# Backward pass of a two-layer decoder step: a new order for the third turn of w1, a shorter regrouping and norm, and one turned tile kept

## Chip, cores and metric

The kernel runs on one core of one Trainium2 chip. The metric is the time of one execution in device microseconds; less is better.

## What is computed

The forward pass and all gradients of two equal layers with shared weights, for two sequences with one new token each. Cut to what matters:

```python
def _A_ref(x, k_cache, v_cache, wq, wo):            # attention, 32 heads on 4 kv heads, 16384 keys
    q = (x @ wq) ...
    p = _softmax(einsum("bhqd,bhkd->bhqk", q, k) * Dh ** -0.5)
    return einsum("bhqk,bhkd->bhqd", p, v) ... @ wo
def _B_ref(x, w1, b1, w2, b2):                      # mlp, D = 1024, F = 3584
    h = _gelu(einsum("bsd,df->bsf", _layernorm(x), w1) + b1)
    return einsum("bsf,fd->bsd", h, w2) + b2
x = x + _A_ref(_layernorm(x), ...); x = x + _B_ref(_layernorm(x), ...)     # layer 0
x = x + _A_ref(_layernorm(x), ...); x = x + _B_ref(_layernorm(x), ...)     # layer 1
# reference(): this output, and its vjp with respect to x, both caches and all weights
```

The caches are 2 x 4 x 16384 x 128 in bf16, 33.6 MB each. Each is read in the forward and in the backward pass of each layer, and a gradient of the same size is written for each.

## The kernel before, in words

All data that is larger than a vector travels in tiles of 128 partitions x 4096 bf16 (1 MB): a quarter of one head's keys or values (32 of 128 columns of keys), four row blocks of wq, wo or w2, or a piece of w1. The vectors of the two tokens are held as columns, 128 partitions x (blocks, 2).

The order of the work is a list written out by hand (`Program.emit`). Each entry names the tiles ("chunks") that it uses. `Program.run` walks through the list once and gives each chunk a slot: 16 slot tiles, and for a time parts of other buffers (two in `e1`, two in `ds1`, one in `late`). A load is issued on SyncE's queue as soon as the list has passed the last use of the slot that it gets; the loads are issued in the order of their first use. So a load waits in the queue for whoever last used its slot, and all later loads wait behind it. `Program.keep` leaves a tile in its slot between two uses where there is room. In the last attention's backward the slots change one after another into staging for outputs.

The stages: attention forward and mlp forward of layer 0, the same of layer 1, then backwards: mlp of layer 1, attention of layer 1, mlp of layer 0, attention of layer 0. In the last stage all the outputs are computed and stored: the gradients of both caches and of the weights, for both layers together, as outer products of 512 columns (`kv_outputs`, `dw_units`), whose PSUM results ScalarE (L276) and VectorE (L279) turn into bf16. `copy_bf` and `cast_out` choose between the two by running sums `st["act"]` and `st["dve"]`; `load_of("dve", 6.0)` adds 6 us to VectorE's sum, so that the next ones go to ScalarE.

A backward product needs the weights with rows and columns exchanged. VectorE's 32x32 transpose of pairs of bf16 ("turning", `turn_rows`, L437, and `turn_cols`, L473) does a quarter of this; the rest is done by a vector spread over four groups of 32 partitions (`spread`, L506 to L507) and 32-column products on the turned tile (`turned_products`, L487). The results then stand in four groups of 32 partitions, and `unquad` (L517 to L529) puts them in order: one copy out of PSUM and 16 small copies of 32 partitions, dealt out to VectorE, ScalarE and GpSimd in turn. Where there is time, weights are instead transposed in place by PE and ScalarE (`turn_here`, L452, L455) and used by plain products (`here_products`, L465).

w1 is turned twice. In the **second turn** (mlp of layer 1, at 415 to 442 us) whole rows are loaded, and `turn_cols` writes four tiles for each half of the rows: `w1t[h][cg]`, half h, column group cg of 896 columns. In the **third turn** (mlp of layer 0, at 633 to 662 us) w1 is loaded again as eight pieces `ws1c` (four row blocks x 896 columns, 896 KB), and `turn_rows` makes eight tiles of them, two halves each: `t1` is the list of the 16 turnings, `p1` the list of the eight product groups.

Around the third turn the list says, before: turnings 0 and 1 inside the attention backward's steps 135 and 137; after its end the last wq products, the layer norm's backward (`attn_in_bwd`: sums, close, rest), turnings 2 and 3, the 28 w2 products (L465) with turnings 4 to 8 among them, `dh0_` (L1533) with the spread, a copy that clears the tile Y (L1540), and then, after each product group, one output unit of w2's gradient (`first`: `y_rows` L1289, `x_rows` L1309, units L1326) and one or two turnings. Then `mlp_in_bwd` (sums, six units, rest), the eight wo products (`wo_prods0`), `do_of`, and the last attention's first steps.

The layer norm's backward (`ln_bwd_terms`, `ln_bwd_sums`, `ln_bwd_rest`) multiplies and sums per partition, sums over partitions with a product by ones (`part_sum`, L594), scales the sums by -1/D, and then needs three steps on (128, 8, 2) for the combination, one for the multiplication by rstd, one for the addition of the residual's gradient, and one for the bf16 copy.

The SyncE wait that the prediction speaks of belongs to `col_to_row` (L617, GpSimd's store): at step 111 of the attention backward of layer 1 the forward output is stored from a slot that a load takes next.

Of the kernel before, what the change touches and what calls it, by code (L numbers as in the profile page):

```python
# [18 lines left out]
LN_EPS = 1e-5  # L19
# [163 lines left out]
def kernel(  # L183
# [468 lines left out]
    def ln_bwd_terms(dy, y):  # L652
        t1 = wrk.tile([128, DJ, 2], F32, name="lb_t1")
        V.tensor_tensor(out=t1[:], in0=dy, in1=y, op=ALU.mult)
        s = small.tile([128, 2, 2], F32, name="lb_s")
        V.tensor_reduce(out=s[:, 0, :], in_=dy.rearrange("p j b -> p b j"), axis=AX.X, op=ALU.add)
        V.tensor_reduce(out=s[:, 1, :], in_=t1[:].rearrange("p j b -> p b j"), axis=AX.X, op=ALU.add)
        return flat(s[:])

    def ln_bwd_sums(dy, y, at=None):  # L660
        return part_sum(ln_bwd_terms(dy, y), 4, at)

    def ln_bwd_rest(ps, dy, y, rstd, twice=False):
        nm = small.tile([128, 2, 2], F32, name="lb_nm")
        V.tensor_scalar(out=flat(nm[:]), in0=ps, scalar1=-1.0 / D, scalar2=None, op0=ALU.mult)
        if twice:
            V.tensor_scalar(out=nm[:, 1, :], in0=nm[:, 1, :], scalar1=1.0 + LN_EPS, scalar2=None, op0=ALU.mult)
        u = wrk.tile([128, DJ, 2], F32, name="lb_u")
        V.tensor_tensor(out=u[:], in0=y, in1=bcast_j(nm[:, 1, :], DJ), op=ALU.mult)
        V.tensor_tensor(out=u[:], in0=u[:], in1=dy, op=ALU.add)  # L670
        V.tensor_tensor(out=u[:], in0=u[:], in1=bcast_j(nm[:, 0, :], DJ), op=ALU.add)
        dx = wrk.tile([128, DJ, 2], F32, name="lb_dx")
        V.tensor_tensor(out=dx[:], in0=u[:], in1=bcast_j(rstd, DJ), op=ALU.mult)
        return dx
# [248 lines left out]
    def mlp_in_bwd(l, fill, gT, parts=False):  # L923
        h = {}

        def sums():
            y, _ = saved[f"m{l}"]
            h["dm"] = wrk.tile([128, DJ, 2], F32, name="dm_sb")
            fill(h["dm"])
            h["ps"] = ln_bwd_sums(h["dm"][:], y[:], half[0, 0] if parts else None)  # L930

        def rest():
            y, r = saved[f"m{l}"]
            dx = ln_bwd_rest(h["ps"], h["dm"][:], y[:], r[:], True)
            gn = vec.tile([128, DJ, 2], F32, name=f"gM{l}")
            V.tensor_tensor(out=gn[:], in0=dx[:], in1=gT[:], op=ALU.add)
            V.tensor_copy(out=gA_all[:, :, 2 * l:2 * l + 2], in_=gn[:])
            return gn

        if parts:  # L940
            return sums, rest
        sums()
        return rest()
# [17 lines left out]
    def wo_bwd_ops(l, k, vb):  # L961
# [3 lines left out]
        def fin():  # L965
            raw = small.tile([128, 8, 2], F32, name="do_raw")
            unquad(raw[:].rearrange("p (c j) b -> p c j b", j=4), acc)
            V.memset(sb[0][:, 64:80], 0.0)
            dve(1.1)
            do_of(l, k, raw[:])  # L970
# [61 lines left out]
    def attn_bwd(l, order, gT, wo_first, outputs=None, mark=None, extra=None):  # L1032
# [127 lines left out]
        if l == 1:  # L1160
            todo = tail + parts
# [9 lines left out]
    def attn_in_bwd(l, gT, dnq):  # L1171
        h = {}

        def sums():
            dn = wrk.tile([128, DJ, 2], F32, name="dn")
            last = sb[0][:, 112:128].rearrange("p (j b) -> p j b", b=2)
            if l == 1:
                V.tensor_copy(out=dn[:], in_=last)
            else:
                V.tensor_tensor(out=dn[:], in0=last, in1=dnq[:], op=ALU.add)  # L1180
            h["dn"] = dn
            h["s"] = ln_bwd_terms(dn[:], vec_y[f"a{l}"][:])
            dve(0.8)

        def close():
            h["ps"] = part_sum(h["s"], 4, half[0, 0] if l == 1 else sb[0][:, 200:])

        def rest():
            dx = ln_bwd_rest(h["ps"], h["dn"][:], vec_y[f"a{l}"][:], vec_r[f"a{l}"][:])
            gn = saved[f"gA{l}"]  # L1190
            V.tensor_tensor(out=gn[:], in0=dx[:], in1=gT()[:], op=ALU.add)
            dve(1.3)
            if l == 1:
                V.tensor_copy(out=gM_all[:, :, 0:2], in_=gn[:])
# [295 lines left out]
    def g3_():  # L1490
        saved["g3"] = mlp_in_bwd(1, lambda dm: unquad(dm[:].rearrange("p (c j) b -> p c j b", j=4), dm_1), gT4)
# [27 lines left out]
    attn_bwd(1, up, lambda: saved["g3"], (None, wo_prods), mark=mark("d1"), extra=extra)  # L1519
# [20 lines left out]
    emit(lambda: S.copy(out=Y.ap.bitcast(I32), in_=wide["n"][:, 0:2].bitcast(I32).to_broadcast([128, CH // 2])), [Y])  # L1540
# [8 lines left out]
    g1p = mlp_in_bwd(0, lambda dm: unquad(dm[:].rearrange("p (c j) b -> p c j b", j=4), dm_0), g2, parts=True)  # L1549
# [47 lines left out]
    emit(lambda: load_of("dve", 6.0))  # L1597
# [49 lines left out]
```

## Time and profile before

| what | value |
|---|---|
| time, median of 3 runs | 1108.54 us (1106.45 to 1108.61) |
| the profiled execution's own time | 1104.69 us |
| its span on the core | 1102.9 us |
| mean granted TensorE clock | 0.927 |
| busy: PE, VectorE, ScalarE, GpSimd | 809.1, 759.6, 492.6, 181.7 us |
| DMA | 448.98 MB, mean 407 GB/s; loads and other hardware queue 351.32 MB, stores 95.48 MB |
| turnings of 128x896 in the third turn | 16, median 1.07 us each |
| loads of 896 KB | 24 by their lines: 16 whole rows of w1 and 8 pieces |

In the profile, a row names the line, the engine, the operation, the tile written and the tiles read, and how many there were. "idle before" is how long the engine did nothing ahead of it, with what ended that. The chain of waits runs back from the last instruction. SyncE does no arithmetic: its rows (SPq) are the issues of loads, and a late issue means that a slot was late. The busy table by stages gives, for each stretch, the busy time of the engines, the granted clock, the DMA engines' busy share and GB/s. Line numbers are those of the kernel before.

### The profile page before, as it was taken

To read this page: it belongs to the slowest core of one execution; us is meant where nothing else is said; L and a number is where in the kernel's file an instruction comes from. 1 tells how busy PE (TensorE), PEld (TensorE's weight loads), DVE (VectorE), ACT (ScalarE), POOL (GpSimd) and SP (SyncE) were. 2 spreads that over 40 slices of the span, in tenths; PEclk is the share of its full clock that TensorE was granted. 3 is DMA by queue.
4 is the path that set the end of the run, shared out by engine and by line. 5 is a ranking of instruction groups with operands and counts; after the bars stand their busy time and mean duration, and the time that the engine had idled before them with its cause. 6 is when DMAs were issued, how large, how long until landed. Compare 5 with 4: busy or idle time off the path is not lost. (4 is left out here: it accounts for less than half of the span.)

```text
span 1102.9 us, 34164 instructions
## 1 busy us (share of the span) xinstructions
PE 809.1 (73%) x14665; PEld 607.6 (55%) x14677; DVE 759.6 (69%) x1472; ACT 492.6 (45%) x1133; POOL 181.7 (16%) x575
## 2 busy tenths in 40 slices
PE   5665666457788657688778678878876986598795
PEld 4554565456777556688778564444443443344453
DVE  5864665168888637755746466979876896598974
ACT  0332222101242321235534326767675776477874
POOL 1000000001000000111211101433332332233330
PEclk9999999999999999988978657989997999799998
DMA  9999999999999999999999998999999999999996
GB/s 372 420 423 421 421 425 423 397 385 413 416 422 421 422 420 383 419 418 421 416 421 419 389 413 307 366 400 424 419 420 425 423 419 422 425 411 420 411 423 269
DMA packets 97932, 448.98 MB, mean 407 GB/s; under 512 B 7624, under 2 KB 11742, under 8 KB 59380
## 3 DMA queue, kind: packets, MB, share of 16 engines
q1 hardware_dynamic: 80532, 351.32, 78.2%
q0 software_dynamic: 17248, 95.48, 21.0%
q8 instruction: 115, 1.88, 0.6%
q14 instruction: 37, 0.30, 0.1%
HBM read 348.15 MB, written 98.62 MB: 405 GB/s over the span
## 5 line engine op out<-in xcount | busy, mean ns | idle before, releaser
L537 DVE STREAM_TRANSPOSE kT<-slot 128x512 int32<-128x512 int32 x436 | 294.1, 695 | 109.5 <-PE sc L550 90.9
L550 PE MATMUL sc<-qbd,kT 128*128 128x32 bf16 x4096 | 263.0, 222 | 11.0 <-DVE kT L537 10.2
L550 PEld LDWEIGHTS <-kT 128*128 128x128 bf16 x4096 | 209.1, 115 | 65.3 <-issue 33.4
L575 PEld LDWEIGHTS <-slot 128*128 128x128 bf16 x3456 | 141.9, 103 | 101.4 <-issue 45.3
L575 PE MATMUL sb<-xt,slot 128*128 128x8 bf16 x3456 | 157.6, 177 | 45.7 <-DMA slot<-in_A_v_cache_dram 23.9
L276 ACT CAST slot<-sc 128x512 bf16<-128x512 f32 x281 | 160.8, 594 | 58.2 <-PE sc L1326 25.0
L1266 PE MATMUL sc<-slot,late 128*128 128x512 bf16 x344 | 127.8, 392 | 23.3 <-DVE slot L279 10.0
L279 DVE CAST slot<-sc 128x512 bf16<-128x512 f32 x172 | 115.2, 678 | 24.5 <-PE sc L1326 10.4
L768 ACT ACTIVATE e<-sc 128x512 bf16<-128x512 f32 x32 | 19.0, 597 | 234.8 <-DVE sc L765 168.6
L276 ACT CAST slot<-sb 128x512 bf16<-128x512 f32 x151 | 89.6, 593 | 37.0 <-PE sb L1326 25.3
L455 ACT COPY slot<-tp 128x512 int32<-128x512 int32 x88 | 50.4, 587 | 106.0 <-PE tp L452 90.3
L452 PE MATMUL tp<-ident,slot 128*128 128x128 bf16 x768 | 74.4, 260 | 11.0 <-DMA slot<-in_A_wq_dram 5.7
L585 ACT COPY xt<-e 32x128 int32<-32x128 int32 x256 | 75.6, 295 | 3.9
L1266 PEld LDWEIGHTS <-late 128*128 128x128 bf16 x512 | 44.5, 98 | 59.5 <-issue 45.7
L1266 PE MATMUL sb<-slot,late 128*128 128x512 bf16 x162 | 63.7, 393 | 7.6 <-DVE slot L279 1.9
L1326 PE MATMUL sc<-slot,late 128*128 128x512 bf16 x155 | 58.7, 401 | 13.8 <-DVE slot L279 9.9
L452 PEld LDWEIGHTS <-slot 128*128 128x128 bf16 x768 | 60.1, 119 | 13.6 <-issue 6.3
L437 DVE STREAM_TRANSPOSE slot<-slot 128x1024 int32<-128x1024 int32 (+1 forms) x46 | 52.9, 1178 | 18.6 <-DMA slot<-in_A_wo_dram 9.1
L279 DVE CAST slot<-sb 128x512 bf16<-128x512 f32 x80 | 54.1, 677 | 9.5 <-PE sb L1266 6.2
L645 POOL TENSOR_TENSOR m_rstd<-ln_vpe,neghalf 128x2 f32<-128x2 f32 x2 | 1.4, 719 | 349.0 <-DVE ln_vpe L643 349.0
L585 POOL COPY xt<-late 32x64 int32<-32x64 int32 x240 | 55.6, 232 | 13.0 <-DVE late L1054 1.9
L585 POOL COPY xt<-ds 32x64 int32<-32x64 int32 x128 | 29.7, 232 | 148.5 <-DVE ds L1054 113.9
(298 smaller groups left out, 1090.9 us busy)
## 6 DMA issues: line engine op xcount, KB each, us to landing
slot<-in_A_k_cache_dram SPq DMA_DIRECT2D x103, 1024.0 KB, 16.4
slot<-in_A_v_cache_dram SPq DMA_DIRECT2D x101, 1024.0 KB, 16.0
out_dram<-slot POOLq DMA_DIRECT2D x55, 1024.0 KB, 14.3
slot<-in_A_wq_dram SPq DMA_DIRECT2D x25, 1024.0 KB, 12.4
slot<-in_A_wo_dram SPq DMA_DIRECT2D x25, 1024.0 KB, 19.7
out_dram<-slot POOLq DMA_DIRECT2D x40, 512.0 KB, 14.1
slot<-in_B_w_dram SPq DMA_DIRECT2D x22, 896.0 KB, 16.4
slot<-in_B_w_dram SPq DMA_DIRECT2D x12, 1024.0 KB, 12.8
```

The lines of the kernel that those rows point to most:

```text
L276: S.copy(out=dst, in_=src)
L279: V.tensor_copy(out=dst, in_=src)
L437: V.transpose(out=t.ap[:, h * nw * 256:(h + 1) * nw * 256].bitcast(I32).rearrange("p (w j m) -> p w j m", j=4, m=32), in_=c.ap[:, 0:4 * nc ...
L452: PE.transpose(tp[:, j * 128:(j + 1) * 128], c.ap[:, off + j * 128:off + (j + 1) * 128], ident[:])
L455: S.copy(out=d.bitcast(I32), in_=tp.bitcast(I32))
L537: V.transpose(out=kT[:].bitcast(I32).rearrange("p (w j m) -> p w j m", w=4, j=4), in_=c.ap[:, (i % 4) * 1024:(i % 4 + 1) * 1024].bitcast(I ...
L550: PE.matmul(sc[:, a0:a0 + 4, :, 2 * (i % 4) + q], lhsT=kv[:, 2 * q + w, :, e], rhs=qbd[:, q_at(g), 2 * w + e], start=(w == 0 and e == 0), ...
L575: PE.matmul(acc, lhsT=c.ap[:, n * 128:(n + 1) * 128], rhs=xv[:, i // 4, t // 2, :, 2 * (i % 4) + t % 2], start=(fresh and i == 0 and t == ...
L585: (GP.tensor_copy if on[t % len(on)] == "g" else S.copy)(out=d[32 * t:32 * t + 32, c0:c0 + cn, j, :], in_=s[32 * j:32 * j + 32, c0:c0 + cn ...
L768: S.activation(out=e_of(l, g)[:, 8 * f:8 * f + 8].rearrange("p a h b -> p h a b"), in_=sc[f][:].rearrange("p h (a b) -> p h a b", b=8), fu ...
L1266: PE.matmul(ps, lhsT=hold["blk"][:, j, :], rhs=flat(qm(w)[:, hf * 4:hf * 4 + 4, :]), start=True, stop=True)
L1326: PE.matmul(ps, lhsT=hold[j // 4 * 4][:, j % 4, :], rhs=Y.ap[:, y_at + c0:y_at + c0 + cn], start=True, stop=True)
```

## The change

- **The third turn in a new order.** Only one turning (one half of the first piece) stands in the attention backward, behind its last step and ahead of the wq products (`after`). Two follow the norm, three stand among the w2 products; the Y copy stands ahead of them; `y_rows` and two turnings stand behind the spread ahead of the first product group, and then one turning follows each of the first six groups.
- **One tile kept.** The tile `w1t[1][3]` of the second turn is used in the last product group of the third turn, too: seven pieces are loaded and turned, 14 turnings instead of 16. The tile keeps its slot from the second turn to the third.
- **A shorter regrouping.** `regroup` takes the place of `unquad` in both `mlp_in_bwd` and in `wo_bwd_ops`: one VectorE multiplication by `quad` out of PSUM, which spreads each value to its place and puts zeros elsewhere, and four f32 products with `quadT` (128 x 32), each into 32 partitions of a PSUM bank. `unquad` stays for `dh_last` and `dn_kept`.
- **A shorter norm.** The terms are multiplied by rstd first, the factor -1/D stands in the matrix of the product (`mean`), the residual's gradient is added while the sum is under way, and behind the sum there are two steps and one for each result (the bf16 one first).
- **Units moved.** Three units instead of six stand between the norm's two parts; one comes behind the wo products and two behind `do_of`. The `load_of("dve", 6.0)` ahead of the last attention goes.

```diff
+    quadT = vec.tile([128, 32], F32, name="quadT")
+    V.tensor_reduce(out=quadT[:], in_=identf[:].rearrange("p (a t) -> p t a", a=4), axis=AX.X, op=ALU.add)
+    mean = vec.tile([128, 1], F32, name="mean")
+    V.memset(mean[:], -1.0 / 1024)
+    meanf = mean[:].to_broadcast([128, 128])
...
+    def regroup(src, at):
+
+        C = src.shape[1]
+        q = small.tile([128, 8, 4, 2], F32, name="uq", bufs=1)[:, 0:4 * C]
+        V.tensor_tensor(out=q, in0=src.rearrange("p c a b -> p (c a) b").unsqueeze(2).to_broadcast([128, 4 * C, 4, 2]),
+                        in1=quad[:].unsqueeze(1).unsqueeze(3).to_broadcast([128, 4 * C, 4, 2]), op=ALU.mult)
+        ps = at[:, 0:8 * C].rearrange("p (c n) -> p c n", c=C)
+        qa = q.rearrange("p (c a) j b -> p c a (j b)", a=4)
+        for a in range(4):
+            PE.matmul(ps[32 * a:32 * a + 32], lhsT=quadT[:], rhs=qa[:, :, a], start=True, stop=True)
+        return ps.rearrange("p c (j b) -> p (c j) b", b=2)
...
+    def ln_bwd_terms(dy, y, rstd, gT, twice=False):
+
+        dr = wrk.tile([128, DJ, 2], F32, name="lb_dr")
+        V.tensor_tensor(out=dr[:], in0=dy, in1=bcast_j(rstd, DJ), op=ALU.mult)
         t1 = wrk.tile([128, DJ, 2], F32, name="lb_t1")
-        V.tensor_tensor(out=t1[:], in0=dy, in1=y, op=ALU.mult)
+        V.scalar_tensor_tensor(out=t1[:], in0=dr[:], scalar=1.0 + LN_EPS if twice else 1.0, in1=y, op0=ALU.mult, op1=ALU.mult)
...
+    def ln_bwd_sums(dr, s, gT, at=None):
+
+        ps = (ob() if at is None else at)[:, 0:4]
+        PE.matmul(ps, lhsT=meanf, rhs=s, start=True, stop=True)
+        V.tensor_tensor(out=dr[:], in0=dr[:], in1=gT, op=ALU.add)
+        return ps
+
+    def ln_bwd_rest(ps, dr, y, outs):
+
         u = wrk.tile([128, DJ, 2], F32, name="lb_u")
...
+        V.tensor_tensor(out=u[:], in0=y, in1=bcast_j(ps[:, 2:4], DJ), op=ALU.mult)
+        V.tensor_tensor(out=u[:], in0=u[:], in1=dr[:], op=ALU.add)
+        for out in outs:
+            V.tensor_tensor(out=out, in0=u[:], in1=bcast_j(ps[:, 0:2], DJ), op=ALU.add)
...
         if l == 1:
-            todo = tail + parts
+            todo = list(after) + tail + parts
...
     for n, c in enumerate(ws1c):
-        t = P.chunk()
-        t1 += turn_rows(c, t, 896)
+        t = w1t[n // 4][n % 4] if n == 7 else P.chunk()
+        t1 += [] if n == 7 else turn_rows(c, t, 896)
...
-    for n, b in enumerate(t1[0:2]):
-        extra.setdefault(135 + 2 * n, []).append(b)
...
-    for b in t1[2:4]:
+    emit(lambda: S.copy(out=Y.ap.bitcast(I32), in_=wide["n"][:, 0:2].bitcast(I32).to_broadcast([128, CH // 2])), [Y])
+    for b in t1[1:3]:
         emit(*b)
...
-        if j % 4 == 3 and 4 + j // 4 < 9:
-            emit(*t1[4 + j // 4])
+        if j % 4 == 3 and j < 12:
+            emit(*t1[3 + j // 4])
...
+    for b in first[0:1] + t1[6:8]:
+        emit(*b)
     for n, b in enumerate(p1):
         emit(*b)
-        for u in first[n + (n > 0):n + 2] + t1[max(9, 8 + 2 * n):10 + 2 * n]:
+        for u in first[n + 1:n + 2] + t1[8 + n + max(0, n - 5):9 + n + max(0, n - 4)]:
             emit(*u)
...
-    for u in first[9:15]:
+    for u in first[9:12]:
         emit(*u)
...
+    wo_prods0 = wo_prods0[:-1] + first[12:13] + wo_prods0[-1:] + first[13:15]
...
-    emit(lambda: load_of("dve", 6.0))
     attn_bwd(0, down, lambda: saved["g1"], (va0, wo_prods0), outputs=outputs, extra=extra)
```

More of the change, by code (lines that the diff above doesn't have):

```diff
@@ L657, in ln_bwd_terms @@
         V.tensor_reduce(out=s[:, 1, :], in_=t1[:].rearrange("p j b -> p b j"), axis=AX.X, op=ALU.add)
[L658 to L667, printed above, removed]
-        u = wrk.tile([128, DJ, 2], F32, name="lb_u")
[L669 to L674, printed above, removed]
+        return dr, flat(s[:]), gT
@@ L921, in mlp_in, with mlp_in_bwd @@
         saved[f"m{l}"] = (y, r)
-    def mlp_in_bwd(l, fill, gT, parts=False):
+    def mlp_in_bwd(l, src, gT, parts=False):
         h = {}
         def sums():
[L927 to L930, printed above, removed]
+            y, r = saved[f"m{l}"]
+            dm = regroup(src, half[0, 1] if parts else ob())
+            h["dr"], s, g = ln_bwd_terms(dm, y[:], r[:], gT[:], True)
+            h["ps"] = ln_bwd_sums(h["dr"], s, g, half[0, 0] if parts else None)
         def rest():
             y, r = saved[f"m{l}"]
-            dx = ln_bwd_rest(h["ps"], h["dm"][:], y[:], r[:], True)
             gn = vec.tile([128, DJ, 2], F32, name=f"gM{l}")
-            V.tensor_tensor(out=gn[:], in0=dx[:], in1=gT[:], op=ALU.add)
-            V.tensor_copy(out=gA_all[:, :, 2 * l:2 * l + 2], in_=gn[:])
+            ln_bwd_rest(h["ps"], h["dr"], y[:], [gA_all[:, :, 2 * l:2 * l + 2], gn[:]])
             return gn
@@ L965, in fin @@
         def fin():
-            raw = small.tile([128, 8, 2], F32, name="do_raw")
-            unquad(raw[:].rearrange("p (c j) b -> p c j b", j=4), acc)
+            raw = regroup(acc, ob())
             V.memset(sb[0][:, 64:80], 0.0)
-            dve(1.1)
-            do_of(l, k, raw[:])
+            dve(0.3)
+            do_of(l, k, raw)
         return turned_pair(ld_wo(k), acc, vb), (fin, ())
@@ L1030, in wq_last_ops, with attn_bwd @@
         return turns, prods
-    def attn_bwd(l, order, gT, wo_first, outputs=None, mark=None, extra=None):
+    def attn_bwd(l, order, gT, wo_first, outputs=None, mark=None, extra=None, after=()):
         kvs = []
@@ L1174, in sums @@
         def sums():
-            dn = wrk.tile([128, DJ, 2], F32, name="dn")
             last = sb[0][:, 112:128].rearrange("p (j b) -> p j b", b=2)
-            if l == 1:
-                V.tensor_copy(out=dn[:], in_=last)
-            else:
+            if l == 0:
+                dn = wrk.tile([128, DJ, 2], F32, name="dn")
                 V.tensor_tensor(out=dn[:], in0=last, in1=dnq[:], op=ALU.add)
-            h["dn"] = dn
-            h["s"] = ln_bwd_terms(dn[:], vec_y[f"a{l}"][:])
+                last = dn[:]
+            h["dr"], h["s"], h["g"] = ln_bwd_terms(last, vec_y[f"a{l}"][:], vec_r[f"a{l}"][:], gT()[:])
             dve(0.8)
         def close():
-            h["ps"] = part_sum(h["s"], 4, half[0, 0] if l == 1 else sb[0][:, 200:])
+            h["ps"] = ln_bwd_sums(h["dr"], h["s"], h["g"], half[0, 0] if l == 1 else sb[0][:, 200:])
         def rest():
-            dx = ln_bwd_rest(h["ps"], h["dn"][:], vec_y[f"a{l}"][:], vec_r[f"a{l}"][:])
             gn = saved[f"gA{l}"]
[L1191 to L1194, printed above, removed]
+            ln_bwd_rest(h["ps"], h["dr"], vec_y[f"a{l}"][:], ([gM_all[:, :, 0:2]] if l == 1 else []) + [gn[:]])
+            dve(0.8)
         res = [(sums, ()), (close, ()), (rest, ())]
@@ L1490, in g3_ @@
     def g3_():
[L1491 removed]
+        saved["g3"] = mlp_in_bwd(1, dm_1, gT4)
     emit(g3_)
@@ L1539 @@
     mark(-1)()
-    emit(lambda: S.copy(out=Y.ap.bitcast(I32), in_=wide["n"][:, 0:2].bitcast(I32).to_broadcast([128, CH // 2])), [Y])
     emit(lambda: load_of("dve", 6.0))
```

7 lines of the change are left out of this document (3 added, 4 removed).

## The prediction

> **What bounds the kernel now.** I read the page's 40 slices first, then the busy times stage by stage, then SyncE's and VectorE's timelines of 595 to 730 us. The DMA engines are 0.9 busy or more in 38 slices of 40, so time can only be won where they run dry or move slowly.
>
> ```profile
> DMA  9999999999999999999999998999999999999996
> GB/s 372 420 423 421 421 425 423 397 385 413 416 422 421 422 420 383 419 418 421 416 421 419 389 413 307 366 400 424 419 420 425 423 419 422 425 411 420 411 423 269
> ```
>
> The deepest dip inside the kernel is slice 25 (307 GB/s, 662 to 689 us): the third turn and what follows it. By stages (columns: stretch and its length; busy us of PE, weight loads, VectorE, ScalarE, GpSimd; granted clock, DMA share, GB/s):
>
> ```profile
> 650.00:662.00 12.00, 10.04 (x246) 8.54 (x245) 8.53 (x10) 5.97 (x9) 1.31 (x3) 0.50 1.02 425
> 662.00:668.00 6.00, 3.82 (x31) 1.80 (x31) 2.67 (x17) 4.15 (x12) 1.64 (x6) 0.50 1.01 413
> 668.00:676.00 8.00, 6.03 (x102) 4.96 (x101) 4.34 (x12) 2.96 (x7) 0.73 (x1) 0.50 1.01 391
> 676.00:684.00 8.00, 7.46 (x73) 3.55 (x70) 4.89 (x8) 7.50 (x17) 0.72 (x2) 0.98 0.34 76
> 692.00:717.00 25.00, 22.88 (x238) 11.55 (x238) 23.24 (x37) 20.15 (x39) 9.38 (x28) 1.00 0.96 359
> 730.00:1080.00 350.00, 283.06 (x3449) 153.99 (x3457) 276.41 (x476) 243.55 (x489) 118.74 (x349) 0.93 1.02 420
> ```
>
> Until 676 the DMA is full, from 676 to 684 it does almost nothing, from 692 to 717 PE (22.88 of 25) and VectorE (23.24) are the bound, and from 730 to 1080 the DMA is again (420 GB/s, share 1.02). SyncE's timeline says why (start, duration, line, load):
>
> ```profile
> 601.84 0.38 SPq L378 DMA_DIRECT2D slot<-in_A_wq_dram  x1
> 609.61 0.33 SPq L373 DMA_DIRECT2D slot<-in_A_v_cache_dram  x1
> ...
> 659.42 0.38 SPq L378 DMA_DIRECT2D slot<-in_A_wo_dram  x1
> 669.31 0.33 SPq L373 DMA_DIRECT2D slot<-in_A_v_cache_dram  x1
> 680.98 0.33 SPq L373 DMA_DIRECT2D slot<-in_A_k_cache_dram  x1
> 688.61 0.38 SPq L378 DMA_DIRECT2D slot<-in_A_wo_dram  x1
> ```
>
> All slots are full by 659. The next come free only as the last attention backward starts, at the end of this chain: the last K tile arrives (635.43), norm, w2 products (641.49), spread, w1 products (651.25 to 661.70), regrouping and norm (to 666.56), wo products (667.39), first V transposes (671.74). Whatever shortens the chain moves the stage up to 717 forward, and with it the full DMA stretch to the end, whose work is the same. Loads taken away before 676 win nothing by themselves: they make the DMA run dry sooner.
>
> **The change, part by part**, against the profiled execution: 1104.69 us, span 1102.9.
>
> *Start of the chain.* One w1 load (896 KB) goes, the first moves behind the last K tile: 0.9175 MB at the 403 to 408 GB/s of 632 to 640 us is 2.27 us earlier for K. But the kept tile takes a slot from the second turn to the third, so all loads in between are issued one release later. Mostly the queue hides that: bytes issued less bytes moved leave 1.8 MB or more queued from 441 to 601 us. It does not at 601.84 to 609.61, where SyncE waits for the slot of the out_0 row, hence for that store (7.3 us by its waits). One more 1 MB load will stand behind this wait: 1.05 MB at 0.405, +2.6 us. K's tile then comes 0.3 us later. There some 0.4 MB were still unmoved at 609.6, up to 1 us to win; around 435 to 440 (254 and 342 GB/s) up to 1 us to lose. I take +0.2 (-0.7 to +1.2).
>
> *Norm of the second attention.* Before, from K: sums at 638.75, gM_all's cast at 641.26. Steps that wait for each other start 0.205 us apart (665.15, 665.35, 665.56 and so on). The copy becomes the multiplication by rstd; of seven steps after the sum, three stay: 4 x 0.205 = 0.82 less. One turning (1.07) now stands ahead on VectorE; its tile comes 2.27 us after K's, so it ends at about 639.0, 0.25 late. Sum -0.55.
>
> *Third turn.* Its VectorE row, and those up to the norm's end:
>
> ```profile
> 654.02 6.23 DVE L437 STREAM_TRANSPOSE slot<-slot 128x896 int32<-128x896 int32 x6 [1.80 <-PE sb L487]
> ...
> 661.74 0.17 DVE L517 COPY uq<-sb 128x16 f32<-128x16 f32 x1 [1.49 <-PE sb L487]
> 661.95 1.03 DVE L525 COPY dm_sb<-uq 32x4 f32<-32x4 f32 x6
> 663.89 0.17 DVE L654 TENSOR_TENSOR lb_t<-dm_sb,m_y 128x16 f32<-128x16 f32 x1 [0.91 <-ACT dm_sb L527]
> ```
>
> Before, nine turnings precede the spread (its multiplication ends at 651.20) and seven follow; after, six precede and eight follow. Eight at 1.04 from 650.65 (0.55 earlier) end at 658.97; then the seventh group's products (0.77), the transposes of an x row (0.40) and the eighth group, which needs no turning (0.94): 661.1 against 661.70. So -0.6 in all up to here, no more than the norm had won: fewer turnings, but PE gets a tile every 2.08 us at the end. The moved Y copy (1.90 on ScalarE, idle for 18.6 us there) and the y rows (1.0 on PE, beside VectorE's 1.09) cost nothing; without that cover, 1.0. The sixth tile's load waits for the sixth turning (646.3) and is needed at 654.8. With a queue nearly empty it takes about 5 us (by the trace's packets 1.4 us from an issue to the first bytes, 2.2 for the bytes, 1.3 from the last byte to the end of a wait on it): no wait.
>
> *Regrouping.* Before, 661.70 to 663.89: 2.19 us for 17 copies on three engines, ScalarE last. After: a multiplication (0.2; the 128x128 ones took 0.25), four f32 products, two hand-overs (0.2). No row has a 32-column f32 product. The 128-column ones start 0.235 us a pass: 8 passes 1.9 us; spread_q's four bf16 products of the same 16 columns: 0.28. I take 0.7, nearer to the latter, doubled for two passes. Sum 1.1, so -1.1 (-1.5 to +0.1). The Trainium skill, "TensorE: Matmul & The Clock Gate", section "LDWEIGHTS (loading the stationary operand)", says that a load costs its columns over 1.2, in ns, whatever the rows. For 32 columns that is an estimated 27 ns, 0.2 us for eight loads instead of my 0.7, and the sum would be 0.5 us lower; no row here shows it.
>
> *Norm of the first mlp.* One step more before the sum (+0.2), three instead of eight after it (-1.03): -0.8. Before, the wo products began at 667.39, 0.8 after gA_all, behind six output units paced by ScalarE's casts (0.49 each). Three remain in front: -0.4. Wo products start 2.9 us earlier.
>
> *Given back.* The other three units now stand around do_of, two of them in front of the transposes whose copy starts the outputs (671.78). They cost 2 x 0.49 on ScalarE and about 0.3 on PE: +1.3. The bias of 6 us against VectorE set before attn_bwd goes; ScalarE was 7.50 of 8 busy from 676 to 684, VectorE 4.89, so some casts move to the idler one: -0.3 (0 to -1).
>
> *Hidden.* The second turn's regrouping and norm (441.7 to 446) lie under a full DMA (416 to 444 GB/s from 440 to 460), the three regroupings of the last attention under 420 GB/s. If that cover went, each would be a gain of 1 to 2 us; no loss. The last norm's savings, some 0.2 us, go unseen between casts.
>
> **Sum:** +0.2 - 0.6 - 1.1 - 0.8 - 0.4 + 1.3 - 0.3 = -1.7; with 0.2 for K's tile in front of an emptier stage (it is issued behind the wo products, not at 680.98), -1.9: 1102.8 for the profiled execution, which lies 3.85 below the median of the runs shown. Against that median: 1108.54 - 1.9 = **1106.6**.
>
> **Rivals.**
>
> *A: the held slot costs more than the chain wins (slower).* Place: the second attention's backward, where at the end some eight slots turn over and seven will. Price: a tile's time, 2.5 us, wherever the queue runs dry: at 601.84 as counted, again at 435 to 440 (0.3 MB left at 433.5) and near 600 (1.8 MB). It decides once what is queued falls below the tile lost plus about 0.6 MB (1.4 us from issue to first bytes), since from 612 on PE waits for one tile after another. Two such holes, +5: 1108.54 - 1.9 + 5 = 1111.6. Against it: 2.3 MB or more at every other release. Chance 0.17.
>
> *B: the win is lost again.* The chain ends 2.9 us earlier, but units, casts and first transposes want the same engine time; ScalarE's 7.50 of 8 speaks for it, VectorE's idle 3 us against. Left: -0.3, 1108.2. Chance 0.25.
>
> *C: K's tile comes earlier.* If the out_0 store lands sooner from a shorter queue, the 2.6 us of delay go and the 2.27 stay: -1.9 - 2.4, 1104.2. Against it: the store is small and need not stand behind the loads. Chance 0.18.
>
> That the load does not go is no case: the changed program has seven of the eight.
>
> **How the numbers follow.** Forecast 0.40 (own range 1105.2 to 1107.8, the bounds of start, regrouping and casts), A 0.17, B 0.25, C 0.18. The range is 1103.0 to 1110.0: it takes in B, C and the forecast, with about 1.5 us by which runs of one kernel differ (1106.45 to 1108.61), and most of A stays out. 0.2% is 2.2 us, about what a measurement of this kernel can tell from no change. Below 1106.3: C and over half of the forecast, 0.40; above 1110.8: A and the forecast's worst end, 0.18; between, 0.42.
>
> **What would show it.** Right: K's last tile within 1 us of 635.4; w1's products end at about 661; regrouping 1.1 us from last product to first multiplication; wo products at 664.5; first outputs' copy at 670.2; the load after 669 is a K tile. Wrong: SyncE idle before 609 longer than one tile; GB/s dips that the slices at 440 to 600 do not have now; four products of over 1.5 us; VectorE waiting on PE in the turn.

## The result and the profile after

Against the kernel before on the same chip the changed kernel took **1103.96 us (median of 17 runs, 1102.02 to 1107.74), the one before 1106.39 (17 runs, 1105.24 to 1109.65)**: 2.4 us less. The ratio is 0.9975, 95% interval 0.9967 to 0.9983, so 1.9 to 3.7 us of 1106.4. The forecast was 1.9 us less (1106.6 against the 1108.54 shown), the range 1103.0 to 1110.0. The time is in it; several terms were not what the prediction said, and the largest errors cancel. Of the 2.6 us by which 1103.96 lies under 1106.6, 2.15 come from the median of before, which fell from 1108.54 (3 runs) to 1106.39 (17 runs).

The profiled execution of the changed kernel took 1105.32 us (span 1103.5), the profiled one of before 1104.69: the one lies above the median of its kernel, the other below, so this pair of traces doesn't show the win. I therefore compare stretches between events, and later means over several kernels that share a part. The page of the changed kernel, the slices:

```profile
DMA  9999999999999999999999999999999999999996
GB/s 371 420 423 420 421 425 422 399 403 397 416 423 421 422 420 373 411 417 421 416 421 398 372 375 392 334 396 423 420 420 424 424 420 420 426 421 421 417 424 249
```

Slice 25 (662 to 690 us) rose from 307 to 392 GB/s, but 22 to 24 (579 to 662 us) fell from 419, 389 and 413 to 398, 372 and 375, and 26 from 366 to 334: the hole has moved, not gone. The same by stages (columns as in the table of before: busy us of the five engines, granted clock, DMA share, GB/s):

```profile
600.00:616.00 16.00, 9.62 (x266) 9.13 (x265) 8.96 (x16) 5.42 (x15) 2.54 (x9) 0.82 0.81 297
616.00:640.00 24.00, 17.26 (x400) 16.56 (x400) 9.66 (x17) 8.47 (x24) 3.71 (x16) 0.71 1.02 416
640.00:650.00 10.00, 7.68 (x238) 7.38 (x237) 7.06 (x17) 1.90 (x1) 0.52 (x1) 0.50 0.86 309
...
662.00:668.00 6.00, 5.14 (x89) 3.17 (x86) 1.82 (x13) 2.54 (x5) 0.73 (x1) 0.50 1.01 411
...
676.00:684.00 8.00, 7.47 (x76) 3.75 (x75) 5.73 (x11) 7.28 (x15) 1.29 (x2) 0.99 1.04 429
684.00:692.00 8.00, 6.92 (x74) 3.52 (x73) 7.42 (x14) 5.92 (x14) 4.51 (x16) 1.00 0.84 296
692.00:717.00 25.00, 22.01 (x224) 10.90 (x224) 21.38 (x34) 19.12 (x36) 7.85 (x25) 0.93 0.93 346
...
730.00:1080.00 350.00, 288.90 (x3490) 155.14 (x3487) 275.77 (x462) 240.31 (x473) 115.90 (x334) 0.92 1.02 422
```

The hole of 676 to 684 us (76 GB/s) is gone, as forecast: a K tile is issued behind the wo products. In its place stand new or deeper ones at 600 to 616 (297 GB/s; 369 before), at 640 to 650 (309; 406 before) and at 684 to 692 (296; 410 before). SyncE's timeline (start, duration, line, load):

```profile
603.23 0.33 SPq L378 DMA_DIRECT2D slot<-in_A_k_cache_dram  x1
610.71 0.38 SPq L383 DMA_DIRECT2D slot<-in_A_wq_dram  x1
...
666.30 0.33 SPq L378 DMA_DIRECT2D slot<-in_A_v_cache_dram  x1
667.16 0.33 SPq L378 DMA_DIRECT2D slot<-in_A_k_cache_dram  x1
687.44 0.38 SPq L383 DMA_DIRECT2D slot<-in_A_wo_dram  x1
```

The wait for out_0's store is as long as before (7.48 us against 7.77), with one load more behind it. Then VectorE in the third turn, and TensorE at its end:

```profile
649.58 1.09 DVE L512 TENSOR_TENSOR kT<-sb,quad 128x896 bf16<-128x896 f32 x1 [0.43 <-PE sb L511]
650.59 8.36 DVE L442 STREAM_TRANSPOSE slot<-slot 128x896 int32<-128x896 int32 x8
662.20 0.23 DVE L540 TENSOR_TENSOR uq<-sb,quad 128x64 f32<-128x64 f32 x1 [3.25 <-PE sb L492]
662.91 0.17 DVE L672 TENSOR_TENSOR lb_dr<-sc,m_rstd 128x16 f32<-128x16 f32 x1 [0.49 <-PE sc L545]
```

```profile
655.63 0.57 PE L492 MATMUL sb<-kT,slot 128*128 128x8 bf16 x16 [0.92 <-issue]
...
661.80 0.36 PE L492 MATMUL sb<-kT,slot 128*128 128x8 bf16 x8 [1.12 <-issue]
662.02 0.59 PE L1337 MATMUL sb<-slot,late 128*128 128x512 bf16 x1
662.53 0.31 PE L545 MATMUL sc<-uq,quadT 128*32 128x16 f32 x8
```

Eight turnings in 8.36 us from 650.59 to 658.95, where 650.65 to 658.97 was forecast. That they agree is luck: the last K tile's dq_all came 1.33 us later than before (637.82 against 636.49), and the way from there to the end of the spread's multiplication was 1.86 us shorter (12.85 against 14.71). The w1 products should have ended at 661.1 and end at 662.16: TensorE stands still for 0.92 and 1.12 us with nothing that the profile shows to wait for. From the last product to the first multiplication of the norm it is 0.75 us (forecast 1.1; 2.19 before).

### The profile page after: what moved, and what is told of

Read it like the earlier page. It is cut to its first block, busy times and chain, and to the rows that moved or that the text cites. A ratio compares the mean times of both kernels' runs of the same rounds, so it can differ in the third digit from the quotient of the medians.

```text
span 1103.5 us, 34173 instructions
## 1 busy us (share of the span) xinstructions
PE 815.1 (74%) x14717; PEld 606.6 (55%) x14717; DVE 754.9 (68%) x1442; ACT 486.1 (44%) x1101; POOL 177.0 (16%) x550
## 3 DMA queue, kind: packets, MB, share of 16 engines
q8 instruction: 115, 1.88, 0.6%
## 5 line engine op out<-in xcount | busy, mean ns | idle before, releaser
L276 ACT CAST slot<-sc 128x512 bf16<-128x512 f32 x291 | 165.7, 593 | 81.0 <-PE sc L1337 44.1
L1277 PE MATMUL sc<-slot,late 128*128 128x512 bf16 x338 | 128.6, 403 | 28.9 <-DVE slot L279 12.6
L279 DVE CAST slot<-sc 128x512 bf16<-128x512 f32 x166 | 111.6, 678 | 25.4 <-PE sc L1277 12.3
L460 ACT COPY slot<-tp 128x512 int32<-128x512 int32 x92 | 52.7, 587 | 113.6 <-PE tp L457 91.3
L276 ACT CAST slot<-sb 128x512 bf16<-128x512 f32 x139 | 82.3, 592 | 25.1 <-PE sb L1337 13.4
L1337 PE MATMUL sc<-slot,late 128*128 128x512 bf16 x170 | 66.0, 407 | 16.9 <-DVE slot L279 9.6
L1277 PE MATMUL sb<-slot,late 128*128 128x512 bf16 x174 | 70.3, 404 | 9.5 <-DVE slot L279 3.7
L279 DVE CAST slot<-sb 128x512 bf16<-128x512 f32 x88 | 59.7, 678 | 15.9 <-PE sb L1277 7.1
```

The costliest lines, as they stand in the source:

```text
L276: S.copy(out=dst, in_=src)
L279: V.tensor_copy(out=dst, in_=src)
L460: S.copy(out=d.bitcast(I32), in_=tp.bitcast(I32))
L1277: PE.matmul(ps, lhsT=hold["blk"][:, j, :], rhs=flat(qm(w)[:, hf * 4:hf * 4 + 4, :]), start=True, stop=True)
L1337: PE.matmul(ps, lhsT=hold[j // 4 * 4][:, j % 4, :], rhs=Y.ap[:, y_at + c0:y_at + c0 + cn], start=True, stop=True)
```

## The experiments

All times are changes against the kernel before on the same chip: ratio of the runs, and that interval in us of 1106.4. E1 to E4 shared one set of runs of before, E5 to E8 another, E9 to E12 a third.

| kernel | median us (runs) | ratio | us against before |
|---|---|---|---|
| changed kernel | 1103.96 (17) | 0.9975 | -2.8 (-3.7 to -1.9) |
| E1 order, short pieces | 1102.48 (11) | 0.9964 | -4.0 (-5.3 to -2.8) |
| E2 kept tile | 1109.56 (11) | 1.0024 | +2.7 (+1.5 to +3.9) |
| E3 order, kept tile | 1109.24 (12) | 1.0018 | +2.0 (+0.6 to +3.4) |
| E4 all, own row | 1101.19 (5) | 0.9948 | -5.8 (-7.4 to -4.0) |
| E5 order, short, own row | 1101.94 (5) | 0.9958 | -4.6 (-6.2 to -3.1) |
| E6 short pieces | 1104.69 (12) | 0.9988 | -1.3 (-2.5 to -0.2) |
| E7 all, six old regroupings | 1106.40 (12) | 0.9999 | -0.1 (-1.3 to +1.1) |
| E8 all, 2 us in the norm | 1106.75 (12) | 1.0002 | +0.2 (-1.1 to +1.5) |
| E9 order | 1106.76 (12) | 0.9998 | -0.2 (-1.7 to +1.2) |
| E10 all, units back | 1104.13 (11) | 0.9975 | -2.8 (-3.9 to -1.7) |
| E11 own row | 1105.89 (12) | 0.9993 | -0.8 (-1.9 to +0.2) |
| E12 all, own row, one turning more ahead | 1100.99 (6) | 0.9942 | -6.4 (-8.2 to -4.6) |

"Short pieces" are the short regroupings and norms, "order" the third turn's new order with the units and the bias, "own row" is explained at E4. The traces of all these kernels, cut at the same events (us; worked out from starts in each trace; "wait" is the last load issued ahead of the wait for out_0's slot, "K" the last K tile's dq_all, "uq" the regrouping's first step, "gA" the end of the step that writes gA_all, "dof" the end of the wo products, "turn" the first V tile's transpose in the last attention, "load" the V load that is issued at about 698, "end" the last instruction):

```
kernel   start-wait  wait-K  K-uq  uq-gA  gA-dof  turn-load  load-end
before     601.84    34.66  25.25   4.83    2.74      26.73    404.39
changed    603.23    34.59  24.37   2.57    2.40      28.96    404.93
E1         602.74    32.63  25.55   2.57    2.40      28.23    404.36
E2         603.00    37.66  24.33   4.83    2.75      26.96    406.26
E3         604.62    35.46  22.96   4.83    1.94      29.05    407.00
E4         602.92    32.23  23.15   2.57    2.40      28.55    404.47
E5         603.06    32.15  25.42   2.57    2.40      27.97    404.35
E6         603.42    36.03  25.32   2.57    3.69      26.77    404.99
E7         603.59    35.17  23.12   2.57    2.40      28.14    404.71
E8         602.57    35.19  23.23   4.92    1.93      28.60    404.25
E9         604.64    32.85  25.67   4.83    1.93      28.52    405.61
E10        603.58    35.38  23.28   2.57    3.78      26.71    405.07
E11        601.45    34.88  25.13   4.83    2.74      26.77    405.71
E12        604.24    32.55  23.95   2.57    2.40      28.83    403.92
```

From dof to turn it is 2.3 to 2.4 us everywhere. The outer columns scatter by 1 to 3 us between like kernels, wait-K and K-uq by up to 1.4 (before and E6; E3 and changed), the others by some tenths.

**Theories.** Chain: the path from the last K tile to the last attention sets the time, and the kept tile is about free. Rival, bytes: the DMA is full, so the load that goes (2.2 us) is the win, and what the chain wins is lost in new holes.

**E1, the kept tile undone.**
```
-        t = w1t[n // 4][n % 4] if n == 7 else P.chunk()
-        t1 += [] if n == 7 else turn_rows(c, t, 896)
+        t = P.chunk()
+        t1 += turn_rows(c, t, 896)
```


> The changed kernel with the kept tile undone: w1's eighth tile of the third turn is loaded and turned again, in the new order; short regrouping and norms stay. Chain theory (the win is the chain's 2.2 us between the last K tile and the wo products; the load that is gone is paid back by the slot that is held): as the changed kernel, 2.4 us under the kernel before (1.5 to 3.0). Bytes theory (the DMA is full from 730 us to the end and nearly full before, so the win is the one load of 896 KB, 2.2 us at 422 GB/s; what the chain wins is lost again in new holes): as the kernel before, within 0.7 us of it.

Measured -4.0 us, more than either theory said: no loss, and 1.2 to 1.5 us better than the changed kernel; since the intervals overlap, this is not certain. **E2, the kept tile alone** (E1's diff the other way, on the kernel before):

> The kernel before with the kept tile alone: the third turn's eighth products read the tile of the second turn, its load and its two turnings go; old order, old regrouping, old norms. Chain theory: the turnings were hidden, so the time stays (within 0.7 us of before), or rises by 1 to 2 us where the held slot makes the holes at 606 and 640 us deeper. Bytes theory: 2.2 us less than before (1.5 to 2.8).

Measured +2.7. With one load less the kernel is slower: the bytes theory is out, and the kept tile is no help as it stands. **E3, the old regrouping and norms** (the functions of before put back, the rest changed):

> The changed kernel with the old regrouping (17 copies) and the old norms; the new order and the kept tile stay. Chain theory: the 1.4 us of the regrouping and the 0.8 us of the norm come back, so about 0.2 to 0.8 us under the kernel before. Bytes theory: as the changed kernel, 2.4 us under before (1.7 to 3.0), its chain being covered by what the DMA still has queued.

Measured +2.0, beyond what either theory said: the short pieces are worth 4.8 us here, not 2.2. The 2.2 left out the six regroupings behind the wo products (E7, below). And some 0.4 us of it lie outside the span: in E3 and E9 the time is on the mean 2.2 us longer than the span on the core, in the other kernels 1.8. **E4, the row of out_0 not in a load slot:**
```
-    extra[111] = [col_to_row(xM1, out_0.rearrange("b s d -> (b s) d"), kind="load")]
+    def out_row():
+        row = va0().rearrange("p w a n -> p (w a n)")[0:DJ, 0:256].rearrange("p (b n) -> p b n", b=2)
...
+        GP.dma_start(out_0.rearrange("b s d -> (b s) d").rearrange("b (j n) -> j b n", n=128), row)
+    extra[111] = [(out_row, ())]
```


> The changed kernel with the row of out_0 written to 512 bytes of another buffer that is idle then, not to a load slot, so that no load waits for that store to land (7.5 us of SyncE, 603.23 to 610.71, in the profile after). Both theories say that the hole of 608 to 614 us (264, 22 and 271 GB/s) closes and K's last tile of the second attention comes 2 to 4 us earlier. Chain theory: the whole rest moves with it, 2 to 3 us under the changed kernel. Bytes theory: the DMA wins the hole's 4 us, but the bytes that it had moved early are then missing at 646 to 650 and 684 to 692 us, so 0.5 to 1.5 us under the changed kernel. If the stall costs nothing, the same time within 0.5 us.

Measured -5.8, that is 3.0 under the changed kernel, as the chain theory said. SyncE's timeline in E4:

```profile
602.92 0.33 SPq L378 DMA_DIRECT2D slot<-in_A_k_cache_dram  x1
603.90 0.38 SPq L383 DMA_DIRECT2D slot<-in_A_wq_dram  x1
605.35 0.33 SPq L378 DMA_DIRECT2D slot<-in_A_v_cache_dram  x1
```

The next load comes after 0.98 us instead of 7.48, and K's last tile 2.4 us earlier (32.23 from wait to K against 34.59). The stage of 640 to 650 us stays as empty as it was:

```profile
640.00:650.00 10.00, 8.78 (x276) 8.39 (x274) 7.74 (x10) 1.36 (x2) 0.52 (x1) 0.50 0.79 281
```

So that hole doesn't lengthen the chain (K to uq is 23.15, among the shortest): all slots are taken there, and SyncE's loads wait for what the chain frees. The edit takes away the wait for the store and one use of a load slot together; no run separates the two.

**E5, E1 and E4 together.**

> The changed kernel with both: w1's eighth tile loaded and turned again, and the row of out_0 in another buffer. Theory of the holes (the kept tile wins its load, 2.2 us, and loses it where the queue runs dry, at 600 to 616 us and at 640 to 652 us; the own row mends the first place alone): the second hole, 2.4 us, is larger than the load, so this runs 0.2 to 1.5 us under the kernel with the kept tile and the own row (1101.2 us), at about 1100.4. Rival (the kept tile costs only where loads wait behind the store of out_0): with that wait gone the load costs its 2.2 us again, so 1103.4 us.

Measured 1101.94 (1100.23 to 1103.54): between the two. Since E4 has 1101.19, the kept tile now wins or is free (intervals overlap; no more can be said). The theory that it loses in the second hole has fallen: from wait to K both take the same (32.23 and 32.15), and from K to uq, where the second hole lies, the kept tile's kernel is 2.3 us shorter (23.15 and 25.42). The two turnings that E5 has more are only the smaller part of that. Their row starts 12.79 us after K's dq_all in E4 and 14.60 in E5: 1.8 us are lost ahead of it, where TensorE stops within the w2 products for 0.68 us in E4 and 2.41 in E5. The w1 products behind the spread take 10.18 and 10.64, so 0.5 more. TensorE's restart in the w2 products and VectorE's row, first in E4, then in E5:

```profile
645.77 0.49 PE L470 MATMUL sb<-gM_all,slot 128*128 128x2 bf16 x13 [0.68 <-issue]
647.95 8.36 DVE L442 STREAM_TRANSPOSE slot<-slot 128x896 int32<-128x896 int32 x8
```

```profile
647.63 0.49 PE L470 MATMUL sb<-gM_all,slot 128*128 128x2 bf16 x13 [2.41 <-issue]
649.81 10.19 DVE L442 STREAM_TRANSPOSE slot<-slot 128x896 int32<-128x896 int32 x10
```

**E6, the short pieces alone** (on the kernel before).

> The kernel before with the short regrouping and the short norms alone: old order, eight loads. Theory (the order of the third turn is worth next to nothing beside them): 3.5 to 4.2 us under the kernel before. Rival (PE gets its tiles too late in the old order, so that what the norm wins ahead of the turn is lost in it, as the working of the prediction had it): the 0.8 us ahead of the turn and the order's share are missing, so 2 to 3 us under before.

Measured -1.3, less than both. The traces name two leaks. Without the order the wo products still stand behind six units, and the stretch gA to dof grows from 2.74 to 3.69. And what the second attention's norm wins is lost in the turn, as the rival said: from K to the end of gM_all it is 4.11 us against 4.94 in before, but TensorE then stops in the w2 products for 2.39 us instead of 1.68, and K to uq is 25.32 against 25.25.

**E7, the old regrouping for the six gradients behind wo products** (`raw = regroup(acc, ob())` back to 17 copies in `unquad`).

> The changed kernel with the old regrouping (17 copies) for the gradients behind the wo products of both attentions alone, six places; the third turn's regrouping and all norms stay short. Theory (the DMA's loss of 1.7 us at 964 to 976 and 1028 to 1036 us in the kernel before, 0.6 in the changed one, comes from these): 1 to 2 us over the changed kernel, and the dips come back. Rival (these regroupings lie under a full DMA, as the prediction had it): no difference, within 0.5 us.

Measured 2.4 to 2.7 us over the changed kernel: not hidden. (E7 puts back three places in the second attention, too, which the prediction did not name; no run separates the two attentions.) The dips are back; stages of before, changed, E7:

```profile
964.00:976.00 12.00, 11.12 (x124) 5.91 (x124) 10.74 (x20) 9.32 (x19) 2.55 (x4) 1.00 1.01 402
1028.00:1036.00 8.00, 6.86 (x95) 3.69 (x92) 7.89 (x13) 6.35 (x14) 2.54 (x6) 1.00 1.01 385
```

```profile
964.00:976.00 12.00, 10.64 (x122) 5.45 (x121) 10.72 (x20) 9.23 (x17) 2.00 (x3) 1.00 1.01 424
1028.00:1036.00 8.00, 7.12 (x118) 4.45 (x117) 7.89 (x13) 6.10 (x13) 3.37 (x11) 1.00 1.01 410
```

```profile
964.00:976.00 12.00, 11.15 (x123) 5.81 (x123) 10.72 (x20) 9.53 (x18) 2.54 (x4) 1.00 1.01 402
1028.00:1036.00 8.00, 6.85 (x97) 3.79 (x96) 7.89 (x13) 6.53 (x13) 2.88 (x7) 1.00 1.01 364
```

The DMA share reads 1.01 in all of them; only the GB/s tell. How much it is worth stays open between two readings: by the runs 2.4 us or more, by the column load-end 1.1 (mean 405.6 of the six traces with the old form, 404.5 of the eight with the short one). E7's own trace is its fastest execution, 1104.03. The dips themselves go with the form in all 14 traces: 365 to 402 GB/s at 964 to 976 us and 364 to 400 at 1028 to 1036 in the six with the old one, 423 to 426 and 410 to 419 in the eight with the short one. An estimate from these means puts the bytes not moved at 1.6 us.

**E8, a delay.** Ten steps that wait for each other in the first mlp's norm.
```
+        for _ in range(late):
+            V.tensor_scalar(out=u[:], in0=u[:], scalar1=1.0, scalar2=None, op0=ALU.mult)
```


> The changed kernel with ten more steps on VectorE in the first mlp's norm, each waiting for the one before (2.0 us at 0.2 a step), so that the wo products begin 2 us later and nothing else changes. Theory of the chain (what lengthens the path from the last K tile to the first transposes of the last attention moves the rest of the program): 2.0 us over the changed kernel (1.4 to 2.6). Rival (engine time behind it is short anyway and takes the delay up, so that the chain is no path): 0 to 0.7 us.

Measured 2.8 to 3.0 over the changed kernel. The steps took 2.35 (uq to gA 4.92), gA to dof gave 0.47 back, so the path grew by 1.9 and the time by no less, within the 1.6 us or so to which the two ratios can be compared. It is the path.

**E9, the order alone** (E3 with E1's diff).

> The kernel before with the new order of the third turn alone (the first tile's turnings behind the last K tile, eight turnings behind the spread, the y rows and the copy ahead, three of the six output units behind the wo products, no bias): eight loads, old regrouping and norms. Theory (the order wins by one load less in front of the last K tile, 2.1 us from the second attention's stall to that tile, whatever the pieces cost): 2.0 to 2.7 us under the kernel before. Rival (its win is small and the rest of it is won only together with the short pieces, as the runs with the kept tile have it, 2.0 against 2.7 us over before): 0.3 to 1.0 us under before.

Measured -0.2 (-1.7 to +1.2): below what the rival said, and the theory is out. It does win 1.8 to 3.2 us ahead of K (32.85 from wait to K; 34.66 in before, 36.03 in E6, which has only short pieces more up to there), and loses it: K to uq +0.4, turn to load +1.8.

**E10, the units and the bias back.**
```
-    for u in first[9:12]:
+    for u in first[9:15]:
...
-    wo_prods0 = wo_prods0[:-1] + first[12:13] + wo_prods0[-1:] + first[13:15]
...
+    emit(lambda: load_of("dve", 6.0))
     attn_bwd(0, down, ...)
```


> The changed kernel with all six output units in front of the wo products again and the bias of 6 us against VectorE back. By the prediction's terms (+0.4 for the units in front, -1.3 for those that then no longer stand behind, +0.3 for the bias): 0.6 us under the changed kernel. Rival (the units in front are the longer stretch, 3.69 us from the norm's end to the wo products' gradient against 2.40, and what stands behind is hidden): 0.8 to 1.5 us over the changed kernel.

Measured as the changed kernel (ratio 0.9975 both), between what the prediction's terms and what the rival said. The stretch gA to dof grows by 1.4, turn to load shrinks by 1.8 against the mean of the nine kernels with three units behind (28.5): moving the units is a swap.

**E11, the own row on the kernel before.**

> The kernel before with the row of out_0 in another buffer alone. Theory (the wait for that store costs each of these kernels, and the kept tile makes it dearer by what one more load behind it is short, about 1 to 2 us): 1.0 to 2.0 us under the kernel before, against 2.8 us in the changed one. Rival (the wait is dear only with the kept tile, since the kernel before had 1.8 MB queued at that point): within 0.5 us of before. Second rival (it costs the same everywhere): 2.8 us under.

Measured -0.8 (-1.9 to +0.2): between the theory and the first rival, and the noise doesn't tell which; the second rival is out. In the trace nothing is won from wait to K (34.88 against 34.66), where E4 won 2.4. So the store's wait is much dearer with the kept tile than without it. **E12, E4 with a seventh turning ahead of the spread** (`j < 16`, and `t1[7:8]` in place of `t1[6:8]`):

> The changed kernel with the row of out_0 in another buffer, and one more turning ahead of the spread (seven, and seven behind it), into the 1.8 us in which VectorE waits for the w2 products (644.5 to 646.3 us in the trace of the kernel with the own row). Theory (behind the spread VectorE's turnings set the pace, 1.04 us each): 0.5 to 1.0 us under the kernel with the own row, 1100.4 us. Rival (PE sets it: eight groups with a unit between them take 9.4 us from 648.0): no difference, 1101.2 us.

Measured 1100.99 against 1101.19: the noise doesn't tell the theory's 0.5 to 1.0 us from nothing. The trace doesn't settle it either: K to uq is 0.8 us longer than in E4 (23.95 and 23.15), but with two stops of TensorE of 0.64 and 0.85 us within the w1 products. E4 and E12 are the fastest of all, 5.8 and 6.4 us under before.

## Why the prediction was right, and where it was wrong

The forecast was right in its main mechanism: what shortens the path from the last K tile to the last attention shortens the time (E8). That the sum of the terms came out near is partly luck, since errors of 1 to 2 us of both signs cancel; and that 1103.96 stands next to rival C's 1104.2 is chance, since C's condition did not come about. Of the signs named, the K tile behind the wo products came (667.16), the regrouping came shorter than said, and K's last tile missed: it arrived at 636.76, more than 1 us from 635.4. The wo products began at 665.24 where 664.5 was forecast; the 2.9 us behind that figure left out the working's own +0.2. The columns of the table, as means over kernels that share the part, against the terms:

- **Start of the chain, +0.2: right, and so were its two halves.** Wait to K: 35.3 with neither (34.66 in before, 36.03 in E6, so known to some 0.7 us only), 32.7 with the order alone (E1, E9), so -2.6 where 2.27 was worked out; 37.66 with the kept tile alone (E2), so +2.3 where 2.6 was; both together 35.2 (changed, E3, E7, E8, E10). The tile behind the store's wait is the cause: with the own row the kept tile costs nothing there (E4 32.23, E5 32.15).
- **Norm of the second attention and third turn, -0.6 together: the step "So -0.6 in all up to here, no more than the norm had won" failed, in both of its parts.** K to uq went from 25.2 (before, E6, E11) to 23.4 (mean of the seven with the new order and the kept tile): -1.8. The norm won 0.83 up to the end of gM_all (4.94 and 4.11 from K in before and E6), but none of it is left at uq: with the old norm E3 has 22.96 and E9 25.67, with the short one E4 23.15 and E1 25.55. The order alone makes K to uq 0.3 longer (E1, E5, E9). What wins is the kept tile: 2.1 with the new order, 0.9 with the old one (24.33 in E2).

  Its two turnings are the smaller part of the 2.1. Behind the spread the w1 products take 10.65 us from first to last in E1, E5 and E9 and 10.00 to 10.34 in E3, E4, E7, E8 and E10, so 0.3 to 0.6 less. Ahead of it, from K to the end of the spread's multiplication, it is 14.8 us in the first three and 12.8 in the seven. There TensorE stops within the w2 products: for 1.57 to 2.41 us in the six kernels that load eight tiles, for 0 to 0.74 in the eight that keep one. The working had no term for this stop; the last section shows what it goes with. The changed kernel's own trace has 24.37, with two more stops of 1.0 us in the w1 products.
- **Regrouping -1.1, norm -0.8: right**; uq to gA -2.26 in all (0.4 more from the products, below).
- **Units and bias, -0.4, then +1.3 and -0.3: right in kind.** gA to dof -0.34, turn to load +1.8; E10 puts the sum at nothing.
- **"Hidden": the step that set the three regroupings of the last attention at nothing failed.** They lay under a mean of 420 GB/s, and the mean hid two dips, at 964 and at 1028 us. Worth 1.1 us by the traces and 2.4 by E7's runs.

These terms add up to about -3.8 (-0.1 - 1.8 - 2.26 - 0.34 + 1.8 - 1.1), and start to wait adds some +0.6 (mean 603.5 with the kept tile, 602.9 without, with a scatter larger than that): -3.2, against -2.4 by the medians and -2.8 by the ratio. The sum is known no better than that.

**Rival A was the true mechanism at its place.** The held slot is dear behind out_0's wait: alone the kept tile costs 2.7 us (E2), with order and short pieces 1.2 (E1), which is within the noise. Three pairs of kernels show it: the own row is worth 0.8 us without the kept tile (E11), 0.6 with order and short pieces (E1 to E5), and 3.0 with the kept tile as well (changed to E4); of these only the last is clear of the noise, and from wait to K the three pairs have +0.2, -0.5 and -2.4. A came out as no slower kernel because the rest of the change won more than forecast. Its other place, 435 to 440 us, was not tried by itself. Rival C's condition did not come about, the store took 5.5 us to land against 5.7. E4 takes the store out of the way by other means: 2.4 us were forecast for C, 3.0 came. Rival B (win lost again) holds for the order alone (E9).

## What to carry to other kernels

Where all slots are full, the stage is as long as its chain, and a hole in the DMA is its shadow: E4 closed the hole that delayed the chain and won 3 us, and left another (281 GB/s over 10 us) that didn't lengthen it. A tile that is kept saves its load and costs a slot; look for the place where the queue waits for a slot in order, above all for one that a small store holds, and move that store before keeping more. A mean over 350 us with a full DMA is no cover: read it in steps of a few us before an edit is set at nothing.

## What the runs showed of the hardware

The store of out_0's row is 4 KB and takes over 5 us from its issue to landing in each of these. The DMA issues of 595 to 612 us in before, changed and E4 (line, KB, us to landing):

```profile
out_dram<-slot POOLq DMA_DIRECT2D x1, 4.0 KB, 5.7
```

```profile
out_dram<-slot POOLq DMA_DIRECT2D x1, 4.0 KB, 5.5
```

```profile
out_dram<-va POOLq DMA_DIRECT2D x1, 4.0 KB, 5.6
```

Within that stretch the DMA moved 374, 325 and 379 GB/s on the mean; the changed kernel's was almost dry near the end of it (22 GB/s from 610 to 612 us), and the store landed hardly sooner. More was not tried.

The four 32-column f32 products were cheaper than I took them, 0.49 us with both hand-overs (VectorE's idle time at 662.91) where 0.9 was taken. The line's own view in the changed kernel, 640 to 680 us (ns: least, median, most):

```profile
L545 PEld LDWEIGHTS sc<-uq,quadT x8: 128/141/154, 662.5 to 662.6; 128*32 128x32 f32 x8
L545 PE MATMUL sc<-uq,quadT x8: 215/226/236, 662.5 to 662.6; 128*32 128x16 f32 x8
```

The rows overlap: the eight loads take 0.20 us together, the eight products 0.31. The Trainium skill, "TensorE: Matmul & The Clock Gate", section "LDWEIGHTS (loading the stationary operand)", gives a load its columns over 1.2 in ns, an estimated 27 here. The rows show 128 to 154 for one load at a granted clock of 0.50, so the trace does not agree for the single load. For the eight it does: 0.20 us against the estimated 0.2, and the sum that it led to (0.5 us less than mine) is near what came (0.4 less).

TensorE's stops that the profile puts down to "issue" go with packets of one DMA queue, the instruction queue q8 (115 packets and 1.88 MB in before, so 16 KB each). From the start of the w2 products to 664 us the 14 traces have 16 stops of over 0.4 us, and in each TensorE starts again 1.2 to 1.6 us after the end of a q8 packet (worked out from the packets' starts and lengths). Stops and packets within the w2 products, us:

```
kernel   stop             packet           GB/s over the w2 products
before   647.47-649.15    646.86-647.74    405
E5       645.22-647.63    645.20-646.16    395
changed  647.75-648.41    646.16-647.12    280
E4       645.09-645.77    643.60-644.56    236
```

In the six kernels that load eight tiles (388 to 408 GB/s over these products) this packet starts 6.0 to 6.2 us after the one before it; in the eight that keep a tile (230 to 289 GB/s) 3.9 to 4.4. So TensorE seems to wait there for its instructions, and longer where the loads fill the DMA; the hole at 640 to 650 us would then shorten the chain. That all 14 traces agree is no proof: no run changed this alone. Not every packet goes with a stop (E2 and E3 have none), and the stops of 0.92 and 1.12 us in the changed kernel's w1 products are not there in E3, E4, E7, E8 and E10, which run the same third turn, so these come and go from one execution to the next.
